# Ten more rank offsets and new scheduling numbers for an attention-then-MoE kernel on one core

## The chip, the cores and the metric

The kernel runs on one core of a Trainium2 chip. The metric is the device time of one launch in microseconds (us); lower is better. The engines are PE (TensorE, matrix products), DVE (VectorE), ACT (ScalarE), POOL (GpSimd) and SP, which here only issues transfers. Each engine takes its instructions strictly in the order in which the program lists them and waits on semaphores for the others.

## The reference

```python
B, H, S, D = 4, 8, 1152, 64
q_pool = q.reshape(B, H, S // 2, 2, D).mean(axis=3)
scores = scale * np.matmul(q_pool, k.transpose(0, 1, 3, 2))      # 576 x 1152 for each head
attn = softmax(scores)                                           # with + 1e-9 under the sum
x = (attn @ v), heads side by side                               # 2304 x 512
h = x @ w_in                                                     # 512 -> 2048
g = h * (1.0 / (1.0 + np.exp(-1.702 * h)))
return g @ w_out                                                 # 2304 x 512
```

## The kernel before

The 32 heads are worked in 16 pairs, four pairs to a batch, and each pair in nine tiles of 128 query rows, so there are 144 tiles, numbered n = 0 to 143; tiles 0 to 35 are the first batch. In seven pairs (0 to 3, 6, 10, 14, the "whole" ones) the softmax rows are kept in f32 and turned by PE; in the other nine they are split into an f16 value and an f16 remainder and turned by a transposing transfer. The program first lists tasks with a name, an engine, a cost, a rank and the tasks that they need. `Plan.order` then walks through time: for every engine it takes, among the tasks that could start within `wait[engine]` of the earliest, the one with the lowest rank, and the tasks are written into the engines' queues in that order. The ranks and waits thus set nothing but the order. A few task kinds can go to either of two engines (`movable`); the planner picks the engine too.

For one tile n the tasks are: S (PE, L581, scores into the one buffer `s` of PSUM); M (DVE, L590, row minimum and copy into `p`, which frees `s` for S of n+1); E (ACT, L597, exp and row sum); D (L602, DVE or POOL, row sum plus 1e-9) and R (DVE, L609, its reciprocal). In a whole pair X (PE, L668) turns a third of the tile into one of two PSUM banks, `o0` and `o1` in turn, and Y (ACT, L238, `pt<-o`) copies it out, so that X must wait for the Y of the X two before it. In the other pairs H (ACT, L238, `hl<-p`) and L (DVE, L617) make value and remainder and T (SP, `pt<-hl`) turns them. Then pv0 and pv (PE, L690 and L652) multiply with v for two tiles at a time.

Beside the first batch the weights are decoded: w_load (SP), w_exp (ACT or DVE, L238 or L242), w_low and w_bits (DVE, L273 and L277), w_sign (ACT, L283), w_mul (POOL, L287), w_sum (PE, L292), then w_hi (ACT or DVE) and w_lo (DVE, L310). The second half (MoE) runs in nine blocks of 256 rows, each in eight steps j: four h tasks (PE, L909, into the one buffer `h`), tanh (ACT, L917), gate (DVE, L923, which frees `h`), g_hi (ACT, L238), g_lo (DVE, L934) and four o tasks (PE, L945). The first tanh waits until all weights are decoded. Attention of later batches and MoE of earlier ones share the engines. Preparation of a pair is q_max, k_max, spread, qk_scale, q_lo, k_lo (DVE) and q_hi, k_hi (ACT).

Of the kernel before, what the change touches and what calls it, by code (L numbers as in the profile page):

```python
# [130 lines left out]
def kernel(  # L131
# [26 lines left out]
    B, H, S, D = q.shape  # L158
# [11 lines left out]


    rank = dict(
        w1=42.737, w1_rate=1.454, w2=148.44, w2_rate=0.024, w1_cut=236.296, w1_cut_rate=0.017,
        w2_cut=142.309, w2_cut_rate=0.125, v_max=140.208, load=3.377, prep=9.462, max=-13.22,
        exp=-50.689, p_hi=-169.539, p_lo=17.316, pv=116.974, x=113.015, recip=3.38, w_tr=-79.718,
        w_ev=15.511,
    )
    movable = dict(DVE=("w_exp", "w_sign", "w_hi"), POOL=("denom",))
    wait = dict(PE=0.074, ACT=0.118, DVE=0.02, POOL=308920.549)
    sizes = dict(  # L180
        qraw=1, qs=1, kraw=1, kn=1, qn=1, kT=2, qT=2, vst=2, vraw=2, vhl0=1, vhl1=1,
        p=3, hl=3, pt=3, ptl=1, xt=2, xf=3, raw=4, th=2, gf=2, g=3, osb=2, s=1, tr=1, pv=1, h=1, o0=1, o1=1,
# [1 line left out]
    plan = Plan(sizes, wait)  # L184
# [42 lines left out]
    def act(n, psum=False, ptr=0):  # L227
        return n / 1200 + (0.051 if psum else 0.092) + 0.093 * ptr

    def dve(n, psum=False, fast=False):  # L230
        return n / (1920 if fast else 960) + (0.065 if psum else 0.068)

    def gps(n):
        return n * 0.0023 + 0.05
# [86 lines left out]
    for i in range(32):  # L321
# [3 lines left out]
        r = rank["w1"] + i / rank["w1_rate"] if i < 16 else rank["w2"] + (i - 16) / rank["w2_rate"]  # L325
# [24 lines left out]
    for c in range(8):  # L350
        for h in range(2):
            e = 2 * (c % 4) + h
            r = rank["w1_cut"] + e / rank["w1_cut_rate"] if c < 4 else rank["w2_cut"] + e / rank["w2_cut_rate"]
# [25 lines left out]
    def k_load(g):  # L379
        t = new("kraw", ("kraw", g.P), [128, 2, KR, D], F32)  # L380
        for a in range(2):
            nc.sync.dma_start(out=t[:, a], in_=k[g.b, 2 * g.pr + a].rearrange("(p r) d -> p r d", r=KR))
# [123 lines left out]
    for b in range(B):  # L506
        first = min(g.n0 for g in pairs if g.b == b)
        for i in range(H):
            r = first - 16 + 1.5 * i if b else -2 + i * 0.25
# [7 lines left out]
        r = first - 2  # L517
# [8 lines left out]
    for g in pairs:  # L526
        n0, G = g.n0, g.P
        now = G == 0
        pe = ("DVE", nc.vector) if now else ("POOL", nc.gpsimd)
        gate = [] if n0 < 10 else [("E", n0 - 10)]  # L530
        r = n0 + rank["prep"]
        qr, qs, kr, kn, qk = ("qraw", G), ("qs", G), ("kraw", G), ("kn", G), ("qn", G)
        kt, qt = ("kT", G), ("qT", G)
        plan.add(("q_load", G), "SP", 2.4, n0 + rank["load"], lambda g=g: q_load(g), gate, take=[("qraw", qr)], dma=1.4)
        plan.add(("k_load", G), "SP", 1.2, n0 + rank["load"] + 0.1, lambda g=g: k_load(g), gate, take=[("kraw", kr)], dma=2.2)
        plan.add(("q_add", G), pe[0], dve(576) if now else gps(576), r, lambda g=g, e=pe[1]: q_add(g, e),
                 [("q_load", G)], take=[("qs", qs)], use=[qr], two=True)
        plan.add(("q_max", G), "DVE", dve(576), r, lambda g=g: q_max(g), [("q_add", G)], use=[qs])
        plan.add(("k_max", G), "DVE", dve(1152), r, lambda g=g: k_max(g), [("k_load", G), ("q_max", G)], use=[kr])
        qa = ("qka", G)  # L540
        plan.add(("rows_max",) + qa, "PE", 0.1, r - 20, lambda g=g, qa=qa: rows_max(T["qk", g.P], qa),
                 [("q_max", G), ("k_max", G)], take=[("tr", qa)])
        plan.add(("spread",) + qa, "DVE", 0.35, r - 20, lambda qa=qa: spread(qa, 2), [("rows_max",) + qa], use=[qa])
        plan.add(("to_all",) + qa, "PE", 0.15, r - 20, lambda qa=qa: to_all(qa, 2), [("spread",) + qa], use=[qa])
        plan.add(("qk_scale", G), "DVE", 0.8, r, lambda g=g: qk_scale(g), [("to_all",) + qa], use=[qa])
        plan.add(("q_hi", G), "ACT", act(1152, ptr=1), r, lambda e, g=g: q_hi(e, g), [("qk_scale", G)],
                 take=[("qn", qk)], use=[qs], two=True, or_on=on("q_hi", DVE=dve(1152, fast=True)))
        plan.add(("q_lo", G), "DVE", dve(576), r, lambda g=g: q_lo(g), [("q_hi", G)], use=[qs, qk], two=True)
        plan.add(("k_hi", G), "ACT", act(1152, ptr=1), r, lambda e, g=g: k_hi(e, g), [("qk_scale", G)],
                 take=[("kn", kn)], use=[kr], two=True, or_on=on("k_hi", DVE=dve(1152, fast=True)))  # L550
        plan.add(("k_lo", G), "DVE", dve(1152), r, lambda g=g: k_lo(g), [("k_hi", G)], use=[kr, kn], two=True)
        plan.add(("q_tr", G), "SP", 3.0, r, lambda g=g: q_tr(g), [("q_lo", G)], take=[("qT", qt)], use=[qk], dma=2.7)
        plan.add(("k_tr", G), "SP", 3.0, r, lambda g=g: k_tr(g), [("k_lo", G)], take=[("kT", kt)], use=[kn], dma=2.7)
        for a in range(2):
            pos = 0 if a == 0 else min(i for i, x in enumerate(g.tiles) if x[0] in "LB")
            r = n0 + (pos + 2 if a == 0 else pos + 3)
            vr, vh = ("vraw", G, a), ("vhl", G, a)
            plan.add(("v_load", G, a), "SP", 0.6, r - 4, lambda g=g, a=a: v_load(g, a),
                     [("E", n0 - 5)] if n0 >= 5 else [("k_load", 0)], take=[("vraw", vr)], dma=1.1)
            if g.whole:  # L560
                continue
            plan.add(("v_hi", G, a), "ACT", act(576, ptr=1), r, lambda e, g=g, a=a: v_hi(e, g, a),
                     [("v_load", G, a), ("vm_scale", g.b)], take=[(f"vhl{a}", vh)], use=[vr],
                     or_on=on("v_hi", DVE=dve(576, fast=True) + 0.06))
# [21 lines left out]
    def row_max(n):  # L586

        g = tile_of[n][0]
        m, p = new("nm", ("nm", n), [128, 1], F32), new("p", ("p", n), [128, 3, 384], F32)
        nc.vector.tensor_scalar(  # L590
            out=p, in0=T["s", n][:, :, 0:384], scalar1=e_s[:, g.P:g.P + 1], scalar2=None, op0=ALU.mult, op1=ALU.min,
            accum_out=m,
        )
# [21 lines left out]
    def p_lo(n):  # L615
        t = T["hl", n]
        nc.vector.scalar_tensor_tensor(  # L617
            out=t[:, 1, :], in0=T["p", n].rearrange("p c f -> p (c f)"), scalar=T["rc", n][:, 1:2],
            in1=t[:, 0, :], op0=ALU.mult, op1=ALU.subtract,
        )  # L620
# [141 lines left out]
    for n, (g, kind, t) in enumerate(tile_of):  # L762
# [5 lines left out]
            use=[("kT", g.P), ("qT", g.P)],  # L768
        )
        plan.add(  # L770
            ("M", n), "DVE", dve(1152, True) + 0.1, n + rank["max"], lambda n=n: row_max(n), [("S", n)],
            use=[("s", n)], take=[("p", ("p", n))],
        )
        plan.add(
# [12 lines left out]
        if g.whole:  # L787
            for c in range(3):
                pb = ("pb", n, c)
                plan.add(("X", n, c), "PE", 0.33, n + rank["w_tr"], lambda n=n, c=c: w_tr(n, c),  # L790
                         [("E", n)] + ([("X", n, c - 1)] if c else []),
                         take=[(f"o{(3 * n + c) % 2}", pb)], use=[("p", n)])
                plan.add(
                    ("Y", n, c), "ACT", act(384, True), n + rank["w_ev"], lambda e, n=n, c=c: w_ev(e, n, c),
                    [("X", n, c)] + ([("Y", n, 0)] if c else []), take=[] if c else take,
                    use=[pb] + ([key] if c else use), or_on=on("w_ev", DVE=dve(384, True)),
                )
        else:
# [17 lines left out]
        else:  # L816
            vs = [("vhl", g.P, e) for e in both]
            ready = [("T", n)] + ([("T", n - 1)] if kind != "L" else []) + [("v_lo", g.P, e) for e in both]
        r = n + rank["pv"]
        if g.whole and kind == "L":  # L820
            plan.add(("pv", g.P, kind, u), "PE", 1.0, r, lambda g=g: w_pv_last(g), ready,
                     take=[("pv", pk)], use=vs + [key])
# [157 lines left out]
            in1=x16a[:, 0, :, 0:256], op0=ALU.mult, op1=ALU.subtract,  # L980
        )

    BIG, R_G = 10 ** 6, -100
    for b in range(B):
        plan.add(("h_scale", b), "DVE", 0.3, -1, lambda b=b: h_scale(b, i_v[:, b:b + 1]),
                 [("w_scale", 0), ("vm_scale", b)])
# [101 lines left out]
```

## Time and profile before

| what | value |
|---|---|
| median of three runs | 843.75 us (842.42 to 844.32) |
| the profiled execution | 842.32 us |
| its span, first to last instruction | 840.5 us |
| granted TensorE clock over the span | 0.997 |
| TensorE busy | 788.9 us |

The time of an execution is the span and 1.8 us around it. A busy time of PE is that of modelled matmul ends, so a busy PE is not always a PE at its peak. Idle time of an engine is charged in the profile to what ended it.

### The profile page before, as it was taken

To read this page: it belongs to the slowest core of one execution; us is meant where nothing else is said; L and a number is where in the kernel's file an instruction comes from. 1 tells how busy PE (TensorE), PEld (TensorE's weight loads), DVE (VectorE), ACT (ScalarE), POOL (GpSimd) and SP (SyncE) were. 2 spreads that over 40 slices of the span, in tenths; PEclk is the share of its full clock that TensorE was granted. 3 is DMA by queue.
4 is the path that set the end of the run, shared out by engine and by line. 5 is a ranking of instruction groups with operands and counts; after the bars stand their busy time and mean duration, and the time that the engine had idled before them with its cause. 6 is when DMAs were issued, how large, how long until landed. Compare 5 with 4: busy or idle time off the path is not lost.

```text
span 840.5 us, 16327 instructions
## 1 busy us (share of the span) xinstructions
PE 788.9 (94%) x6403; PEld 516.9 (61%) x6403; DVE 647.3 (77%) x1196; ACT 604.0 (72%) x964; POOL 117.0 (14%) x174
## 2 busy tenths in 40 slices
PE   1699999996999999999999999999999999999997
PEld 0356556554666775766667756665666666666664
DVE  5898998989999979799989699988886883222221
ACT  3599999997987887688768888786788873232322
POOL 2233233331110111100110100111100010000000
PEclk9999999999999999999999999999999999999999
DMA  8986847458989968989999479999993581000001
GB/s 290 271 200 224 217 126 184 120 144 161 212 153 204 214 137 153 185 180 236 205 202 195 113 125 193 178 196 204 171 199 57 114 148 35 14 13 13 18 8 26
DMA packets 296365, 126.96 MB, mean 151 GB/s; under 512 B 267360, under 2 KB 277600, under 8 KB 296288
## 3 DMA queue, kind: packets, MB, share of 16 engines
q1 hardware_dynamic: 296288, 125.92, 70.6%
q8 instruction: 50, 0.82, 0.4%
q14 instruction: 27, 0.22, 0.1%
HBM read 54.53 MB, written 4.72 MB: 70 GB/s over the span
## 4 chain that ended last, share of the span: by engine, by line
PE 60%; DVE 19%; DMA 8%; ACT 7%; issue 5%; SPq 1%; POOL 0%; DVEq 0%; ACTq 0%; POOLq 0%
PE h L909 15%; PE o L945 14%; PE s L581 10%; PE o L668 7%; PE pv L690 7%; DVE p L590 6%; DVE hl L617 5%; PE pv L652 4%; DMA pt<-hl 3%; DMA raw<-in_moe_w_in_dram 2%; ACT p L597 2%; DMA ptl<-hl 2%; ACT pt L238 1%; PE h L292 1%; ACT hl L238 1%
## 5 line engine op out<-in xcount | busy, mean ns | idle before, releaser
L590 DVE TENSOR_SCALAR_CACHE_REDUCE p<-s,e_s 128x1152 f32<-128x1152 f32 x144 | 203.4, 1412 | 17.3 <-PE s L581 11.1
L597 ACT ACTIVATE p<-p,nm 128x1152 f32<-128x1152 f32 x144 | 180.3, 1252 | 34.1 <-DVE p L590 27.2
L945 PE MATMUL o<-wbuf,g 128*128 128x512 f16 x864 | 204.4, 379 | 0.5 <-DVE wbuf L310 0.5
L909 PEld LDWEIGHTS <-wbuf 128*128 128x128 f16 x1728 | 167.0, 98 | 37.4 <-issue 4.0
L581 PE MATMUL s<-kT,qT 128*128 128x384 f16 (+1 forms) x960 | 166.8, 329 | 14.1 <-DVE p L590 12.8
L945 PEld LDWEIGHTS <-g 128*128 128x128 f16 x864 | 82.5, 98 | 87.0 <-issue 5.1
L581 PEld LDWEIGHTS <-qT 128*128 128x128 f16 (+1 forms) x960 | 83.3, 100 | 73.5 <-issue 27.8
L617 DVE SCALAR_TENSOR_TENSOR hl<-p,rc,hl 128x1152 f16<-128x1152 f32 x81 | 114.0, 1410 | 10.8 <-ACT hl L238 10.4
L238 ACT ACTIVATE hl<-p,rc 128x1152 f16<-128x1152 f32 x81 | 100.9, 1247 | 24.8 <-DMA pt<-hl 8.2
L909 PE MATMUL h<-x16a,wbuf 128*128 128x256 f16 x960 | 117.5, 273 | 0.0
L917 ACT ACTIVATE th<-h,t_s 128x512 f32<-128x512 f32 x72 | 49.1, 682 | 87.4 <-PE h L909 87.1
L923 DVE SCALAR_TENSOR_TENSOR gf<-th,h 128x512 f32<-128x512 f32 x72 | 49.2, 684 | 81.2 <-ACT th L917 80.6
L668 PE MATMUL o<-idf,p 128*128 128x128 f32 x567 | 87.4, 283 | 5.5 <-ACT pt L238 4.1
L909 PE MATMUL h<-wbuf 128*128 128x256 f16 x768 | 91.9, 273 | 0.0
L668 PEld LDWEIGHTS o<-idf,p 128*128 128x128 f32 x567 | 63.0, 142 | 35.6 <-ACT pt L238 16.4
L238 ACT ACTIVATE pt<-o 128x384 f32<-128x384 f32 x168 | 75.9, 486 | 7.8 <-PE o L668 6.9
L690 PE MATMUL pv<-pt,vraw 128*64 128x256 f32 x504 | 71.8, 389 | 0.0
L934 DVE SCALAR_TENSOR_TENSOR g<-gf,g 128x512 f16<-128x512 f32 x72 | 50.0, 694 | 20.4 <-ACT g L238 20.2
L652 PE MATMUL pv<-pt,vhl 128*64 128x256 f16 x972 | 64.8, 279 | 0.6 <-DMA pt<-hl 0.6
L238 ACT ACTIVATE g<-gf 128x512 f16<-128x512 f32 x72 | 44.9, 624 | 25.6 <-DVE gf L923 25.2
L652 PEld LDWEIGHTS <-vhl 128*64 128x64 f16 x972 | 52.6, 111 | 13.7 <-issue 12.2
L690 PEld LDWEIGHTS pv<-pt,vraw 128*64 128x64 f32 x504 | 35.4, 136 | 24.8 <-issue 9.5
(91 smaller groups left out, 717.6 us busy)
## 6 DMA issues: line engine op xcount, KB each, us to landing
kraw<-in_k_dram SPq DMA_DIRECT2D x32, 288.0 KB, 4.1
vst<-in_v_dram SPq DMA_DIRECT2D x32, 288.0 KB, 3.8
vraw<-in_v_dram SPq DMA_DIRECT2D x32, 288.0 KB, 3.4
qraw<-in_q_dram SPq DMA_DIRECT2D x32, 256.0 KB, 3.8
raw<-in_moe_w_in_dram SPq DMA_DIRECT2D x16, 512.0 KB, 5.6
raw<-in_moe_w_out_dram SPq DMA_DIRECT2D x16, 512.0 KB, 3.9
out_dram<-osb SPq DMA_DIRECT2D x16, 256.0 KB, 2.3
pt<-hl SPq DMA_TRANSPOSE x72, 5.3
```

What stands on the lines that cost most here:

```text
L238: nc.scalar.activation(out=out, in_=in_, func=ACTF.Copy, scale=1.0 if scale is None else scale)
L581: nc.tensor.matmul(out=ps[m, c, 0:384], lhsT=st, rhs=T["kT", g.P][:, o:o + 3].rearrange("p r c -> p (r c)"), start=(l == 0), stop=(l == 1),)
L590: nc.vector.tensor_scalar(out=p, in0=T["s", n][:, :, 0:384], scalar1=e_s[:, g.P:g.P + 1], scalar2=None, op0=ALU.mult, op1=ALU.min, accum_o ...
L597: nc.scalar.activation(out=p, in_=p, func=ACTF.Exp, bias=T["nm", n], scale=-1.0, accum_out=sm)
L617: nc.vector.scalar_tensor_tensor(out=t[:, 1, :], in0=T["p", n].rearrange("p c f -> p (c f)"), scalar=T["rc", n][:, 1:2], in1=t[:, 0, :], o ...
L652: nc.tensor.matmul(out=ps[64 * o:64 * (o + 1), :], lhsT=T["vhl", g.P, a][:, c, a if m is None else m], rhs=pt[:, l * KR + c, :], start=(i ...
L668: nc.tensor.transpose(ps[:, 128 * i:128 * (i + 1)], T["p", n][:, c, 128 * i:128 * (i + 1)], idf)
L690: nc.tensor.matmul(out=ps[64 * o:64 * (o + 1), :], lhsT=T["vraw", g.P, a][:, c], rhs=pt[:, c, :], start=(c < 2), stop=(c >= KR - 2),)
L909: nc.tensor.matmul(out=h[:, e, :], lhsT=w1(2 * j + e, l, kk), rhs=x_rhs(blk, m, kk), start=(kk == 0 and l == 0 and m == 0), stop=(kk == KD ...
L923: nc.vector.scalar_tensor_tensor(out=gf, in0=T["th", blk, j], scalar=1.0, in1=T["h", blk, j].rearrange("p e n -> p (e n)"), op0=ALU.add, o ...
L934: nc.vector.scalar_tensor_tensor(out=g[:, 1].rearrange("p e n -> p (e n)"), in0=T["gf", blk, j], scalar=2.0 ** -16, in1=g[:, 0].rearrange( ...
L945: nc.tensor.matmul(out=o, lhsT=g[:, l, e, 128 * t:128 * (t + 1)], rhs=w2(fc, m), start=(fc == 0 and l == 0 and m == 0), stop=(fc == KFF - ...
```

## The change

The change rewrites the numbers of the planner and gives it new offsets. Four task kinds get a second offset that counts only for later tiles: the products with v (`pv_b`), the score moves M (`max_b`) and the preparation (`prep_b`) from tile 36 on, the remainders L (`p_lo_b`) from tile 72 on. The rank of the MoE's tanh, gate, g_hi, g_lo and output copies, -100 before, becomes `g`, -122.8. All other offsets and the four waits have new values; that of POOL falls from 308920.549, by which POOL always took the lowest rank, to 5.641.

```diff
     rank = dict(
-        w1=42.737, w1_rate=1.454, w2=148.44, w2_rate=0.024, w1_cut=236.296, w1_cut_rate=0.017,
...
+        recip=-32.2016, w_tr=-43.1433, w_ev=20.3844, g=-122.7884, pv_b=3.9697, max_b=3.9962,
+        p_lo_b=54.4429, prep_b=0.0995,
     )
...
-    wait = dict(PE=0.074, ACT=0.118, DVE=0.02, POOL=308920.549)
+    wait = dict(PE=0.029, ACT=0.037, DVE=0.022, POOL=5.641)
...
-        r = n0 + rank["prep"]
+        r = n0 + rank["prep"] + (rank["prep_b"] if n0 >= 36 else 0.0)
...
-            ("M", n), "DVE", dve(1152, True) + 0.1, n + rank["max"], lambda n=n: row_max(n), [("S", n)],
+            ("M", n), "DVE", dve(1152, True) + 0.1, n + rank["max"] + (rank["max_b"] if n >= 36 else 0.0), lambda n=n: row_max(n), [("S", n)],
...
-            plan.add(("L", n), "DVE", dve(1152) + 0.06, n + rank["p_lo"], lambda n=n: p_lo(n), [("H", n)],
+            plan.add(("L", n), "DVE", dve(1152) + 0.06, n + rank["p_lo"] + (rank["p_lo_b"] if n >= 72 else 0.0), lambda n=n: p_lo(n), [("H", n)],
...
-        r = n + rank["pv"]
+        r = n + rank["pv"] + (rank["pv_b"] if n >= 36 else 0.0)
...
-    BIG, R_G = 10 ** 6, -100
+    BIG, R_G = 10 ** 6, rank["g"]
```

No task is added or dropped and none changes its shape. Of the tasks with two engines, D stands 99 times on DVE and 45 times on POOL (56 and 88 before; in tiles 0 to 35 it is 22 on DVE, 8 before), w_exp 9 times on DVE (7) and w_hi once (2). In the changed kernel the line numbers are higher by one.

On DVE, at the hand-over from the first batch to the first MoE step, the rows of before run from M of tile 39 (`p_2242`) to M of tile 41 (`p_2330`); `gf` is the gate, `qn0` and `kn` are q_lo and k_lo, `vhl1` is v_lo of pair 4.

```order
L590 TENSOR_SCALAR p_2242,nm_2241<-s_2166,e_s_76 128x1152
L248 TENSOR_SCALAR pow_2247<-tr_2183 128x2
...
L501 SCALAR_TENSOR_TENSOR vhl1_2239<-vraw_2205,s_v_83,vhl1_2239 128x9x64
L602 TENSOR_SCALAR rc_2275<-sum_2266 128x1
L590 TENSOR_SCALAR p_2279,nm_2278<-s_2253,e_s_76 128x1152
...
L445 SCALAR_TENSOR_TENSOR qn0_73<-qs_2088,s_qk_74,qn0_73 128x9x64
L459 SCALAR_TENSOR_TENSOR kn_2282<-kraw_2069,s_qk_74,kn_2282 128x18x64
L617 SCALAR_TENSOR_TENSOR hl_2234<-p_2140,rc_2190,hl_2234 128x1152
L923 SCALAR_TENSOR_TENSOR gf_2324<-th_2301,h_2192 128x512
L590 TENSOR_SCALAR p_2330,nm_2329<-s_2285,e_s_76 128x1152
```

The same place of the changed kernel runs from M of tile 39 (`p_2228`) to M of tile 40 (`p_2398`).

```order
L591 TENSOR_SCALAR p_2228,nm_2227<-s_2186,e_s_76 128x1152
...
L618 SCALAR_TENSOR_TENSOR hl_2194<-p_2121,rc_2166,hl_2194 128x1152
L603 TENSOR_SCALAR rc_2267<-sum_2255 128x1
...
L924 SCALAR_TENSOR_TENSOR gf_2276<-th_2265,h_2159 128x512
...
L618 SCALAR_TENSOR_TENSOR hl_2234<-p_2155,rc_2205,hl_2234 128x1152
L935 SCALAR_TENSOR_TENSOR g_2294<-gf_2276,g_2294 128x512
L618 SCALAR_TENSOR_TENSOR hl_2303<-p_2228,rc_2267,hl_2303 128x1152
L924 SCALAR_TENSOR_TENSOR gf_2341<-th_2320,h_2287 128x512
L446 SCALAR_TENSOR_TENSOR qn0_73<-qs_2099,s_qk_74,qn0_73 128x9x64
L460 SCALAR_TENSOR_TENSOR kn_2339<-kraw_2074,s_qk_74,kn_2339 128x18x64
L591 TENSOR_SCALAR p_2398,nm_2397<-s_2238,e_s_76 128x1152
```

Before, qk_scale (`pow`), v_lo, M of tile 40, q_lo, k_lo and one L stand ahead of the first gate; now they stand behind it, two gates pass before M of tile 40, and M of tile 40 has moved from ahead of the first gate to behind the second.

On PE at the same hand-over the rows of before are these; `h` is h of a step j, `s` is S, `pv` with `vhl` the products of pair 4, and `o0` with `wbuf` the first o task.

```order
L909 MATMUL h_2192<-x16a_71,wbuf_70 128x256
...
L581 MATMUL s_2253<-kT_1928,qT_1887 64x384
...
L581 MATMUL s_2285<-kT_1928,qT_1887 128x384
...
L652 MATMUL pv_2308<-pt_2237,vhl0_2188 64x256
...
L581 MATMUL s_2354<-kT_1928,qT_1887 128x384
...
L909 MATMUL h_2372<-x16a_71,wbuf_70 128x256
...
L945 MATMUL o0_2419<-wbuf_70,g_2332 128x512
```

In the changed kernel PE has this order there.

```order
L910 MATMUL h_2159<-x16a_71,wbuf_70 128x256
...
L582 MATMUL s_2238<-kT_1866,qT_1832 64x384
...
L910 MATMUL h_2287<-x16a_71,wbuf_70 128x256
...
L653 MATMUL pv_2322<-pt_2215,vhl0_2203 64x256
...
L910 MATMUL h_2359<-x16a_71,wbuf_70 128x256
...
L582 MATMUL s_2403<-kT_1866,qT_1832 128x384
...
L910 MATMUL h_2413<-x16a_71,wbuf_70 128x256
...
L946 MATMUL o0_2433<-wbuf_70,g_2294 128x512
```

Where the first step's h was followed by S of tiles 40, 41 and 42 and only then by the second step's h, S of tile 40 is now followed by the h of the second and third step, with the products of pair 4 between them, and S of tile 41 comes behind.

On PE in the first batch, tiles 32 to 34, the rows of before are these; `p_1852`, `p_1901` and `p_1940` are the three tiles, and a row ending in x3 is one X.

```order
L668 MATMUL o0_1974<-idf_67,p_1852 128x128 x3
L668 MATMUL o1_1983<-idf_67,p_1901 128x128 x3
L668 MATMUL o0_1994<-idf_67,p_1901 128x128 x3
L668 MATMUL o1_1998<-idf_67,p_1901 128x128 x3
L668 MATMUL o0_2005<-idf_67,p_1940 128x128 x3
```

In the changed kernel the same tiles are `p_1858`, `p_1908` and `p_1956`, and the rows run so.

```order
L669 MATMUL o0_1964<-idf_67,p_1858 128x128 x3
L293 MATMUL h_1038<-raw_1681,ones_68 128x512
...
L669 MATMUL o1_1987<-idf_67,p_1908 128x128 x3
L669 MATMUL o0_1994<-idf_67,p_1908 128x128 x3
L691 MATMUL pv_1999<-pt_1905,vraw_1550 64x256 x6
...
L669 MATMUL o1_2014<-idf_67,p_1908 128x128 x3
L669 MATMUL o0_2021<-idf_67,p_1956 128x128 x3
```

Five X in a row are now broken up by a w_sum, an S (left out behind it) and a product with v. Counted over tiles 0 to 35, an X has less than 1 us of other PE work between itself and the X before last 19 times of 106 before, and 6 times of 106 now.

## Rows read from the trace of the kernel before

**Rows 1.** The page: span, busy us (share) by engine, and two groups (mean ns | idle).
```profile
span 840.5 us, 16327 instructions
PE 788.9 (94%) x6403; PEld 516.9 (61%) x6403; DVE 647.3 (77%) x1196; ACT 604.0 (72%) x964; POOL 117.0 (14%) x174
...
L597 ACT ACTIVATE p<-p,nm 128x1152 f32<-128x1152 f32 x144 | 180.3, 1252 | 34.1 <-DVE p L590 27.2
...
L690 PE MATMUL pv<-pt,vraw 128*64 128x256 f32 x504 | 71.8, 389 | 0.0
```

**Rows 2.** By stage: length, busy PE, PEld, DVE, ACT, POOL, granted clock, DMA.
```profile
45.00:185.00 140.00, 134.35 (x1035) 81.13 (x1034) 126.08 (x269) 132.65 (x252) 46.76 (x62) 1.00 0.66 177
...
192.50:211.30 18.80, 10.71 (x89) 7.59 (x90) 18.66 (x31) 14.51 (x20) 2.89 (x4) 0.91 0.93 179
211.30:450.00 238.70, 234.75 (x2039) 157.49 (x2038) 220.07 (x395) 191.21 (x283) 27.70 (x46) 1.00 0.97 190
...
682.00:840.50 158.50, 153.79 (x1114) 103.57 (x1111) 47.76 (x69) 50.45 (x79) 2.13 (x4) 0.99 0.14 29
```

**Rows 3.** Groups by line on PE, 45 to 185 us: busy, mean ns | idle before.
```profile
L668 PE MATMUL o<-idf,p 128*128 128x128 f32 x300 | 46.3, 284 | 5.2 <-ACT pt L238 4.1 <-ACT ptl L238 0.6
```

**Rows 4.** Waits from 189 to 213 us: who waited, us in total, times, longest.
```profile
PE s L581 <- DVE p L590: 8.1, 4, 2.7
```

**Rows 5.** Timeline of PE, last of these waits: start, duration, [idle before <-releaser].
```profile
209.69 1.14 PE L581 MATMUL s<-kT,qT 128*128 128x384 f16 x6 [1.81 <-DVE p L590]
```

**Rows 6.** Timeline of DVE at the hand-over: start, duration, line.
```profile
194.81 0.78 DVE L249 TENSOR_SCALAR pow<-pow 128x2 int32<-128x2 int32 x1
...
196.81 0.81 DVE L501 SCALAR_TENSOR_TENSOR vhl<-vraw,s_v,vhl 128x576 f16<-128x576 f32 x1
197.54 0.15 DVE L602 TENSOR_SCALAR rc<-sum 128x1 f32<-128x1 f32 x1
197.60 1.41 DVE L590 TENSOR_SCALAR_CACHE_REDUCE p<-s,e_s 128x1152 f32<-128x1152 f32 x1
...
199.34 0.80 DVE L445 SCALAR_TENSOR_TENSOR qn<-qs,s_qk,qn 128x576 f16<-128x576 f32 x1
200.06 1.41 DVE L459 SCALAR_TENSOR_TENSOR kn<-kraw,s_qk,kn 128x1152 f16<-128x1152 f32 x1
201.39 1.41 DVE L617 SCALAR_TENSOR_TENSOR hl<-p,rc,hl 128x1152 f16<-128x1152 f32 x1
202.72 0.68 DVE L923 SCALAR_TENSOR_TENSOR gf<-th,h 128x512 f32<-128x512 f32 x1
203.31 1.41 DVE L590 TENSOR_SCALAR_CACHE_REDUCE p<-s,e_s 128x1152 f32<-128x1152 f32 x1
...
204.65 0.69 DVE L934 SCALAR_TENSOR_TENSOR g<-gf,g 128x512 f16<-128x512 f32 x1
...
206.71 1.28 DVE L310 SCALAR_TENSOR_TENSOR wbuf<-wbuf,s_w 128x1024 f16<-128x1024 f32 x1
207.90 0.41 DVE L751 SCALAR_TENSOR_TENSOR xf<-pv,xt 64x256 f32<-64x256 f32 x1
```

**Rows 7.** Groups by line on DVE, whole span, as in rows 3.
```profile
L602 DVE TENSOR_SCALAR rc<-sum 128x1 f32<-128x1 f32 x33 | 4.9, 148 | 10.3 <-ACT p L597 10.2
L249 DVE TENSOR_SCALAR pow<-pow 128x2 int32<-128x2 int32 (+1 forms) x22 | 4.3, 195 | 0.8
L602 DVE TENSOR_SCALAR w_r<-sum 128x1 f32<-128x1 f32 x23 | 3.5, 150 | 12.7 <-ACT p L597 12.5
```

**Rows 8.** Timeline of POOL at the hand-over, columns as in rows 5.
```profile
194.52 2.04 POOL L287 TENSOR_TENSOR wbuf<-raw 128x512 f32<-128x512 f32 x2 [6.29 <-ACT raw L283]
```

**Rows 9.** The chain that ended last, three pieces of PE: start, us, line.
```profile
251.22 1.65 PE pv L652 x27
...
268.39 2.62 PE h L909 x24
...
272.07 2.59 PE o L945 x12
```

More of the change, by code (lines that the diff above doesn't have):

```diff
@@ L172 @@
     rank = dict(
-        w1=42.737, w1_rate=1.454, w2=148.44, w2_rate=0.024, w1_cut=236.296, w1_cut_rate=0.017,
-        w2_cut=142.309, w2_cut_rate=0.125, v_max=140.208, load=3.377, prep=9.462, max=-13.22,
-        exp=-50.689, p_hi=-169.539, p_lo=17.316, pv=116.974, x=113.015, recip=3.38, w_tr=-79.718,
-        w_ev=15.511,
+        w1=12.6806, w1_rate=0.751823, w2=102.8954, w2_rate=0.051016, w1_cut=181.2675,
+        w1_cut_rate=0.049742, w2_cut=112.9397, w2_cut_rate=0.539374, v_max=96.827, load=-1.2316,
+        prep=-3.3578, max=-0.5482, exp=-171.1792, p_hi=0.457, p_lo=3.294, pv=28.4174, x=41.7521,
+        recip=-32.2016, w_tr=-43.1433, w_ev=20.3844, g=-122.7884, pv_b=3.9697, max_b=3.9962,
+        p_lo_b=54.4429, prep_b=0.0995,
     )
     movable = dict(DVE=("w_exp", "w_sign", "w_hi"), POOL=("denom",))
-    wait = dict(PE=0.074, ACT=0.118, DVE=0.02, POOL=308920.549)
+    wait = dict(PE=0.029, ACT=0.037, DVE=0.022, POOL=5.641)
     sizes = dict(
```

## The prediction

> **What bounds the kernel now.** I read the page first, then busy times by stage, then the waits of the stages in which PE is not full. PE is busy 788.9 us of 840.5 [rows 1], and the change adds no PE instruction, so the time can only move by PE's idle and held-up time. The stages tell where that lies [rows 2]. In the last 158.5 us there is little but MoE: PE 153.8, DVE 47.8. From the sixth block's h of step 5 on, PE's two orders are the same task for task, so nothing moves there. From 211.3 to 450 PE is busy 234.8 of 238.7 and DVE 220.1: a full PE with a nearly full DVE under it. In the first batch, 45 to 185, ACT is busy 132.7 of 140, DVE 126.1 and PE 134.4; the most loaded engine there is ACT, and PE's 5.7 idle us are almost all X waiting for the copy of the X before last [rows 3]. The weak place is the hand-over from first batch to MoE, 192.5 to 211.3: PE busy 10.7 of 18.8, DVE 18.66. The waits say who holds PE: S on M, four times, 8.1 us [rows 4], the last of them 1.81 us [rows 5]. There is one `s` buffer, so PE, which has S of tile 40, 41, 42 and 43 next in its queue, stands still until DVE has come to the M before, and DVE's queue has preparation and remainders between the M's. MoE work that could fill PE stands behind these S's, and its first gate ends only at 203.4 [rows 6]. Up to the scores of tile 2 PE's two orders are the same, and DVE's up to the first D, so the empty start stays as it is.
>
> **The hand-over, priced by DVE's starts.** On a full DVE the distance from one start to the next is what an instruction costs, less than its duration. The starts give [rows 6]: M 1.34 (203.31 to 204.65), L 1.33, k_lo 1.33, q_lo 0.72, v_lo 0.73, gate and g_lo 0.59 each, w_lo 1.19, D 0.06 (197.54 to 197.60). The five small steps of qk_scale cost 0.9 at the 0.195 of such a step [rows 7]; here four of them took 2.0 (194.81 to 196.81), with two w_mul of POOL beside them [rows 8]. What moves behind the first gate is thus qk_scale 0.9 to 2.0, v_lo 0.73, M 1.34, q_lo 0.72, k_lo 1.33 and L 1.33: 6.4 to 7.5 us. That it comes earlier is not itself the gain, since what is put off must still be done; the gain is in what PE has to do meanwhile.
>
> I count PE's new waits from the end of the first gate as zero. Behind it DVE has R (priced like D), qk_scale, L, g_lo, L and the second gate: 0.1 + 0.9 + 1.33 + 0.6 + 1.33 + 0.6 = 4.8. Then q_lo, k_lo, g_lo, one addition of products (0.4, its duration at 207.90), v_lo and M of tile 40: 5.1, so that M ends at 9.9. PE has an h step of 2.62 and pv of 1.65 [rows 9]: with 0.2 for the semaphore (an estimate) it is done at 4.5, waits 0.5 for the second gate, does the next h until 7.6 and waits 2.4 for M of tile 40. S (0.97, from 209.69 to the next start) with two h tasks and two o tasks (a quarter of 2.62 and of 2.59 each) ends at 13.6; M of tile 41 has ended at 13.1 (gate, w_lo, D, M behind 9.9), so no wait. Ahead of the gate PE's queue behind S of tile 39 holds the rest of pair 3's products (18 of 504 matmuls of 71.8 us, 2.56 [rows 1]), one h task, S of tile 40 and two small products (0.3): 4.5. DVE's queue from M of tile 39 through the gate holds M, v_lo, L and the gate (4.0), an addition and a division (0.8), three small scales and D (0.7): 5.5. A wait of 1.0. Carried on in the same way, S of tile 46 waits 0.7 for an M that has w_lo, v_lo and a sum of products ahead of it. Together 0.5 + 2.4 + 1.0 + 0.7 = 4.6 in place of 8.1: **-3.5 us**. Bounds: 0, if what was put off holds PE up later by as much, and -8.1, if none of the new waits comes.
>
> **X in the first batch.** X's on one bank that stand close wait for ACT: 5.2 us of idle PE [rows 3]. Close pairs (under 1 us of work between) fall from 19 to 6. If the idle time goes with them, 13/19 of 5.2 is 3.6 us; if ACT with its 95% sets the pace anyway, it is nothing. I take half, as DVE and PE are both within 10% of full too: **-1.8**.
>
> **D on DVE.** In the first batch 14 more D's stand on DVE. By starts one costs 0.06 [rows 6], by duration 0.15 [rows 7]: +0.9 to +2.1 us on an engine that has 14 us idle there, and I take 0.9 in full: **+0.9**. The Trainium skill, "Perfetto Trace Analysis", section "Optimizing Scalar/DVE Operations", says that a small operation's profiled latency is about twice the time for which it holds the engine, which it puts at about 60 ns on SBUF. By that rule the 14 cost 0.8 and the sum below would be -4.5, by the durations 2.1 and -3.2; the starts at 197.54 and 197.60 agree with the rule. Behind tile 35 there are 29 more, 1.7 us by starts. Until 450 they lie beside 18.6 us of idle DVE [rows 2], later beside more, and PE is the full engine there: 0; without that cover, at most 1.7. The moves of w_exp (two more on DVE) and w_hi (one less there) about cancel. POOL loses 43 instructions of an engine that is busy 14% [rows 1]: 0, but see the third rival.
>
> **Sum.** -3.5 - 1.8 + 0.9 = -4.4 against the profiled execution, 840.5 in span and 842.32 in all: 837.9. That execution lies 1.4 under the median of the runs shown, so for the median I give 843.75 - 4.4 = 839.4, rounded to 839.5. The likeliest case's own range is 837 to 842.
>
> **Rivals.**
> *The gain is given back (no change).* Behind the hand-over DVE is busy 220 of 239 us and does the same tasks; the preparation and remainders put off for two gates must be done before the products of pair 4 and the scores of pair 5. If DVE, not PE, sets the pace up to 450, PE's head start ends as waits of S on M there. For it: DVE's 92%. Against it: PE idles only 3.9 us in 239 there, so PE is the fuller. Time 842 to 845.
> *D holds DVE up (slower).* A D on DVE waits in order for its E, and M, L and gates queue behind it, S behind M. The D's on DVE already show 22.7 us of idle DVE before them [rows 7], 0.4 for each of 56, though mostly where DVE has time to spare. In the new order 22 instead of 8 stand in the first batch, half of them with less than 2 us of DVE work between M and D, while E itself takes 1.25 [rows 1] and a read of its sum behind M. It decides if ACT starts its E's more than about 0.4 us late. Then 14 new waits of 0.5 to 0.8 put 7 to 11 us on the first batch and X's gain is gone; less the 3.5 of the hand-over that is 847 to 851. For it: ACT is the fullest engine there.
> *More than forecast.* POOL's wait of 308920 made it hold its rank order, with D's waiting for E ahead of w_mul and x_lo; 43 of these D's are gone, and w_sum and w_mul of the last weights come earlier. If the first batch gives all of 3.6, D hides, and the hand-over gives 4.7 because no w_mul slows qk_scale (1.2 more): 843.75 - 3.6 - 4.7 = 835.4. The same section of the Trainium skill says that GpSimd and VectorE share an SBUF read port, so that moving operations between the two might not help, and by that rule DVE's work would also get shorter where POOL's leaves. The trace shows such a stretch only beside w_mul (0.78 for a 0.195 step), none beside a D.
> *The planner's order does not come out on the chip.* The trace is full of waits of 0.2 to 0.8 us that no order shows, and a new order of 3,300 tasks can lose a few us anywhere in 180 to 680: this widens every case above by about 2 us.
>
> **How the numbers follow.** Two measurements of this kernel can be told apart from about 0.2%, 1.7 us. Chances: forecast 0.44, more than forecast 0.12, given back 0.20, D holds DVE up or losses elsewhere 0.24. Faster by over 0.2% (under 842.1) holds the first two, less some of the forecast's upper edge, plus some of the third: 0.55; within, 0.20; slower 0.25. The range runs from just under the time of the third rival to the near end of the second's, 834.5 to 847; beyond it lie about half of the 0.24 and a little of the 0.12, together under 0.2.
>
> **What the new profile would show.** Right: S's waits on M between the first batch's end and the first o fall from 8.1 to about 5 us, the first gate comes before its 203.4; idle before `o<-idf,p` in the first batch falls under 3 us; the idle before D on DVE stays near 0.4 for each; the last MoE blocks run as before, only earlier. Wrong: S of tiles 5 to 35 waiting on M behind D's; PE idle from 211 to 450 rising above 7 us; or the first gate later than 203.

## The result and the profile after

The changed kernel is slower: 853.77 us median (852.33 to 855.82, 4 runs) against 844.04 (842.42 to 844.38, 4 runs) of the kernel before on the same chip, a ratio of 1.0131 (95% interval 1.0116 to 1.0147). The ratios here are the record's estimates over all runs; the two medians alone give 1.0115, and a share below that is a difference from 1.0131 would be some 0.15% smaller by medians. The forecast was 839.5, its range ended at 847. The profiled execution of the changed kernel took 852.42 us, with a span of 850.6, 10.1 more than [rows 1]. Its line numbers are one higher than those of before.

From the page of the changed kernel, against [rows 1]:

```profile
span 850.6 us, 16276 instructions
...
PE 794.2 (93%) x6403; PEld 517.5 (61%) x6403; DVE 655.7 (77%) x1240; ACT 604.1 (71%) x963; POOL 95.9 (11%) x131
```

DVE does 8.4 us more than before and POOL 21.1 less. By stage, columns as in [rows 2]:

```profile
45.00:185.00 140.00, 134.38 (x1053) 83.39 (x1050) 126.64 (x280) 131.68 (x249) 36.62 (x47) 1.00 0.63 177
192.50:211.30 18.80, 13.47 (x106) 9.44 (x106) 17.47 (x33) 14.13 (x20) 0.67 (x1) 0.86 0.86 166
211.30:450.00 238.70, 228.04 (x1940) 150.20 (x1939) 219.22 (x390) 186.35 (x275) 21.70 (x32) 1.00 0.92 183
245.00:272.00 27.00, 22.67 (x211) 16.47 (x210) 26.77 (x49) 22.60 (x30) 0.64 (x2) 1.00 0.85 146
```

The first batch is as it was. In the hand-over PE is busy 2.8 us more. Then 211 to 450 loses 6.7 us of PE, 3.8 of them in the 27 us from 245, where DVE is full; PE's idle time from 211 to 450 is 10.7 us, 4.0 before. The same 27 us in the kernel before:

```profile
245.00:272.00 27.00, 26.42 (x211) 17.92 (x210) 26.33 (x40) 21.76 (x30) 0.38 (x2) 1.00 0.91 174
```

DVE is full there too, but PE is as well. So "DVE full" alone is not what tells the two apart. The waits of PE in the changed kernel, 189 to 213 us (against [rows 4]):

```profile
PE s L582 <- DVE p L591: 2.1, 1, 2.1
PE tr L427 <- DVE cd L424: 2.1, 1, 2.1
PE tr L419 <- DVE xf L724: 0.9, 1, 0.9
```

S waits on M 2.1 us in place of 8.1; two waits in the maxima of pair 5 (`tr`, 3.0 us) are new. The waits of PE from 225 to 305, first the changed kernel, then before, which has one wait over 0.2 us in all that time:

```profile
PE s L582 <- DVE p L591: 5.2, 5, 2.2
PE pv L653 <- DMA pt<-hl: 1.2, 1, 1.2
PE h L910 <- DVE gf L924: 1.0, 2, 0.9
PE o L946 <- DVE rc L603: 0.8, 1, 0.8
```

```profile
PE o L945 <- DVE wbuf L310: 0.5, 1, 0.5
PE tr L426 <- DVE cd L423: 0.2, 1, 0.2
```

To compare executions whose tasks stand in another order I use PE's backlog: at a time t, t less the work that PE has done, each PE task counted at the lower quartile of its kind's start-to-start distances in the kernel before; shown is the backlog less that of before, in us. One execution scatters by some 2 us: the changed kernel and "transfers_ahead" below have one order up to 240 us, and differ by 2.0 at 230.

```
t                     180   210   230   250   270   300   440   720
changed               1.0  -2.2  -0.1   1.0   5.1   7.7   9.3  10.1
early_to_s46          0.9   0.9   0.9   0.2   3.8   7.7  10.1  10.0
late_to_s46           1.4  -0.9   1.3   6.0   5.4   5.5   5.9   4.5
transfers_ahead       1.8  -0.4   1.9   3.3   5.8   6.6   9.0   9.6
d_back_behind         1.4  -1.9  -0.3  -0.1   4.2   5.7   7.7   7.1
d_back_transfers      0.8  -2.6  -0.8  -0.7   2.5   2.7   4.2   4.4
light_vector          0.6  -2.7  -0.9  -0.3   2.5   2.7   4.2   5.7
w_lo_ahead            1.1  -2.1   0.1   1.2   2.9  10.0  13.0  13.8
```

So the loss is not at the hand-over, where PE is 2.2 us ahead at 210. That lead is gone by 230, and between 230 and 300 arise 7.8 us of 10.1 (PE's busy time in these 70 us, 62.47 us against 69.14, says 6.7).

### The profile page after: what moved, and what is told of

It reads as the page before. It is cut to its first block, busy times and chain, and to the rows that moved or that the text cites. A ratio compares the mean times of both kernels' runs of the same rounds, so it can differ in the third digit from the quotient of the medians.

```text
span 850.6 us, 16276 instructions
## 1 busy us (share of the span) xinstructions
PE 794.2 (93%) x6403; PEld 517.5 (61%) x6403; DVE 655.7 (77%) x1240; ACT 604.1 (71%) x963; POOL 95.9 (11%) x131
## 4 chain that ended last, share of the span: by engine, by line
PE 53%; DVE 27%; DMA 6%; issue 6%; ACT 5%; SPq 1%; ACTq 0%; DVEq 0%
PE h L910 13%; PE o L946 12%; PE s L582 9%; DVE hl L618 7%; PE o L669 7%; DVE p L591 7%; PE pv L691 6%; PE pv L653 3%; DMA pt<-hl 3%; DMA ptl<-hl 2%; ACT p L598 2%; DVE g L935 1%; DVE qk L410 1%; DVE gf L924 1%; DVE xf L752 1%
## 5 line engine op out<-in xcount | busy, mean ns | idle before, releaser
L591 DVE TENSOR_SCALAR_CACHE_REDUCE p<-s,e_s 128x1152 f32<-128x1152 f32 x144 | 203.0, 1410 | 12.3 <-PE s L582 7.9
L618 DVE SCALAR_TENSOR_TENSOR hl<-p,rc,hl 128x1152 f16<-128x1152 f32 x81 | 117.8, 1457 | 9.0 <-ACT hl L239 8.8
```

The costliest lines, as they stand in the source:

```text
L591: nc.vector.tensor_scalar(out=p, in0=T["s", n][:, :, 0:384], scalar1=e_s[:, g.P:g.P + 1], scalar2=None, op0=ALU.mult, op1=ALU.min, accum_o ...
L618: nc.vector.scalar_tensor_tensor(out=t[:, 1, :], in0=T["p", n].rearrange("p c f -> p (c f)"), scalar=T["rc", n][:, 1:2], in1=t[:, 0, :], o ...
```

## Experiments

Each kernel holds both sets of numbers; `plan.order(0)` gives the order of before and `plan.order(1)` the changed one, each as a list of tasks with their engines, and `mixed` is the list that is written into the queues. `put(a, b)` moves task a to just ahead of b. Nothing else differs, and every ratio is to the kernel before on the same chip (its median 842.6 to 843.3 in these runs). Lines of their profiles are ten higher than before's: S is L591, M L600, D L612 (in light_vector thirteen behind its edit).

**Where the loss lies.** The two orders are cut at S of tile 46 and crossed; the diff is that of late_to_s46, and in early_to_s46 a and b are exchanged.

```diff
-    mixed = plan.order(1)
+    a, b = plan.order(1), plan.order(0)
+    cut = [t["name"] for t, _ in a].index(("S", 46)) + 1
+    done = {t["name"] for t, _ in a[:cut]}
+    mixed = a[:cut] + [x for x in b if x[0]["name"] not in done]
```

> The changed order up to S of tile 46, then the order of before for all that is left. Theory 1 (the order behind S of tile 46, about 230 to 300 us, is itself too tight for DVE): PE was level with before at that point (0.1 us ahead) and the loss comes later, so 843 to 846. Rival (a debt: what is put off for the first gates, 6.2 us of DVE work against 4.2, can't be made up by any order behind it): 849 or more.

> The mirror: the order of before up to S of tile 46, then the changed order. Theory 1: the loss of some 8 us between 230 and 300 us, and the 2 behind it, come back without the first batch's 1.5: 850 to 854. Rival (debt): nothing was put off, so 843 to 846.

Measured: 846.93 us, ratio 1.0054 (1.0036 to 1.0071), and 849.04, 1.0081 (1.0052 to 1.0110). Both lie between the two theories, and neither holds alone. With the order of before up to S of tile 46, and so with nothing put off, the changed order behind it still lost 7.5 us from 250 to 300 (the table): that piece of order is bad by itself. But the changed hand-over also leaves a debt: with the order of before behind it, what had been put off came at once and the backlog rose by 4.7 between 230 and 250.

**The D's.** In the two orders 69 D's stand on different engines: 56 move to DVE and 13 to POOL. Only the engines are changed back, or across.

```diff
+    place = {t["name"]: e for t, e in plan.order(0)}
+    mixed = [(t, place[t["name"]] if t["name"][0] == "D" else e) for t, e in plan.order(1)]
```

> The changed order with each D on the engine where it stood before (43 go back to POOL; every instruction keeps its place in the program). If the D's on DVE hold DVE up (the third rival): 843 to 847. If they cost only their own 0.06 to 0.15 us beside a full PE (theory 1): 850 to 854.

> The order of before with the D's on the engines of the changed kernel (43 more on DVE), nothing else moved. If the D's hold DVE up: 848 to 853. Theory 1: 843 to 846, the first batch's 14 costing 1 to 2 us at most.

Measured: 849.10 us, 1.0080 (1.0052 to 1.0108), and 846.52, 1.0050 (1.0033 to 1.0067). The D's cost about 0.5% in either order. Then the two halves of the 69, with `t["name"][1] >= 36` or `< 36` added to the condition:

> The changed order with the D's of tile 36 and later on the engines of before, those of the first batch as changed. The prediction gave these D's (29 more on DVE, net) a cost of 0, since PE was the full engine there. If they are the cost, nearly all of the 4.7 us of the run with every D put back comes off: 848 to 851. If the cost lies in the first batch: 853 to 855.

> The mirror: the D's of the first batch (14 more on DVE, net) on the engines of before, the later ones as changed. If the later ones are the cost: 852.5 to 855. If the first batch's are: 848 to 851.

Measured: 849.59 us, 1.0077 (1.0062 to 1.0092), and 853.25, 1.0122 (1.0094 to 1.0150). The cost lies behind tile 35. On DVE from 230 to 305 us, first the changed kernel, then with every D put back:

```profile
L603 DVE TENSOR_SCALAR rc<-sum 128x1 f32<-128x1 f32 x6 | 0.8, 138 | 0.0
L603 DVE TENSOR_SCALAR w_r<-sum 128x1 f32<-128x1 f32 x4 | 0.6, 148 | 1.4 <-ACT p L598 1.4
```

```profile
L612 DVE TENSOR_SCALAR rc<-sum 128x1 f32<-128x1 f32 x3 | 0.4, 137 | 0.0
L612 DVE TENSOR_SCALAR w_r<-sum 128x1 f32<-128x1 f32 x2 | 0.3, 143 | 0.6 <-ACT p L607 0.6
```

Ten D's and 1.4 us of waiting for E stand where there were five and 0.6: 0.7 us of duration and 0.8 of waiting, 1.5 together, against the 1.8 by which the backlog grows less from 230 to 300 with the later D's back (6.0 in place of 7.8). At 720 the two are 3.0 apart, so part of the cost comes later; where was not followed.

**A late remainder of the weights.** In the changed kernel w_lo 6 1 ran at 266.5 us, 245.3 before, and the o's of step 5 cannot start without it.

```diff
+    put(("w_lo", 6, 1), ("g_lo", "h", 0, 5))
+    for i in range(4):
+        put(("o", 0, 5, i), ("S", 50))
+    put(("w_hi", 7, 0), ("E", 50))
+    put(("w_hi", 7, 1), ("tanh", "h", 1, 0))
+    put(("w_lo", 7, 0), ("R", 52))
+    put(("w_lo", 7, 1), ("D", 53))
```

> The changed order with one remainder of the weights, w_lo 6 1, moved on VectorE from between L of tile 50 and M of tile 53 to just ahead of g_lo of step 5 (there about 20 us earlier, as in the order of before), the four o's of step 5 moved on PE from behind S of tile 54 to ahead of S of tile 50, and w_hi and w_lo of the last weights each one place up. Theory 2 (that remainder kept the o's off PE, and S then waited on M with nothing in between): the idle PE of 252 to 283 us, 6.3 us in five gaps, falls by 3 to 5, and the ratio to before from 1.013 to 1.007 to 1.010 (849 to 852). Rival (VectorE is simply full there, whatever PE has to do): the ratio stays at 1.013 (853 to 855).

Measured: 855.38 us, 1.0144 (1.0124 to 1.0163). The theory fell. Up to 270 PE does gain (2.9 in the table against 5.1), but by 300 it is 2.3 worse than the changed kernel. SP's longest wait between 235 and 290 us in this run says what came instead:

```profile
SPq L480 <- DVE qn L455: 7.3, 1, 7.3
```

The same edit with the D's put back, then with the order of before up to w_bits of the last piece in place of the changed first batch, alone and with both other edits:

> The edit of the w_lo run, and each D on the engine where it stood before. If the two costs are apart from each other, the 4.7 us of the D's come off as well: 844 to 847. If both are one thing (a VectorE that is full between 230 and 290 us), only the larger shows: 848 to 850.

> The order of before up to w_bits of the last piece of the weights (183 us), the changed order behind it. The first batch lay 1.4 us behind before at 180 us: if that is its whole share, 852 to 853. If the stretch behind lives from what the changed first batch got ready (the weights, that is), it gets worse: 854 or more.

> All three: the first batch as before, w_lo 6 1 ahead, the D's as before; what is left of the change is the hand-over and the order of the tiles and steps behind it. If the three costs add up (1.4, 3 to 5, 4.7) it comes to 842 to 845, the hand-over's 3 us still given back; below 842 if the hand-over's gain is kept as well.

Measured: 851.21 us, 1.0107 (1.0081 to 1.0133); 850.02, 1.0098 (1.0061 to 1.0135); 848.42, 1.0070 (1.0051 to 1.0089). None of the three lies in a range that was expected. The D's come off beside the w_lo edit as well (1.0107 against 1.0144). The first batch's share is not settled by the second, whose interval is wide.

**SP's queue.** That wait is there in the changed kernel too. SP's queue, 233 to 275 us: start, duration, line; L632 is T, L471 q_tr, the transfer that turns `qn` (pair 6):

```profile
233.24 14.88 SPq L632 DMA_TRANSPOSE pt<-hl  x4
254.26 2.68 SPq L471 DMA_TRANSPOSE qT<-qn  x1
257.03 3.36 SPq L632 DMA_TRANSPOSE pt<-hl  x1
260.50 2.87 SPq L467 DMA_TRANSPOSE kT<-kn  x1
263.42 2.80 SPq L632 DMA_TRANSPOSE pt<-hl  x1
266.27 1.05 SPq L494 DMA_DIRECT2D vraw<-in_v_dram  x2
267.42 3.66 SPq L632 DMA_TRANSPOSE ptl<-hl  x1
```

From 248.1 to 254.3 SP issues nothing, since q_tr waits for q_lo 6; behind it stand T of tile 47, k's transfer, T of tile 48, two loads and T of tile 49 (`ptl`). After 254 the queue is packed, and some 25 us later that reaches PE. ACT, DVE and PE, in this order:

```profile
275.25 1.25 ACT L239 ACTIVATE hl<-p,rc 128x1152 f16<-128x1152 f32 x1 [2.08 <-DMA ptl<-hl]
276.41 0.61 ACT L239 ACTIVATE g<-gf 128x512 f16<-128x512 f32 x1
```

```profile
277.06 0.69 DVE L935 SCALAR_TENSOR_TENSOR g<-gf,g 128x512 f16<-128x512 f32 x1 [2.09 <-ACT g L239]
277.67 2.56 DVE L618 SCALAR_TENSOR_TENSOR hl<-p,rc,hl 128x1152 f16<-128x1152 f32 x1
```

```profile
282.40 0.81 PE L582 MATMUL s<-kT,qT 128*128 128x384 f16 x4 [2.21 <-DVE p L591]
```

H of tile 52 waits for a transfer (T of tile 49, late) to give back an `hl` buffer, g_hi stands behind H, g_lo behind g_hi, L and M behind g_lo, and S of tile 56 waits 2.2 us. A wait at the head of SP's queue is nothing special: in the kernel before SP issues nothing but one load from 244.6 to 250.7, with the same T's behind q_tr, and PE has no wait over 0.5 from 225 to 305. But there q_tr goes out 3.5 us and T of tile 49 4.5 us earlier:

```profile
250.74 3.20 SPq L470 DMA_TRANSPOSE qT<-qn  x1
...
262.92 2.44 SPq L631 DMA_TRANSPOSE ptl<-hl  x1
```

The edit touches SP alone:

```diff
+    put(("v_load", 6, 0), ("q_tr", 6))
+    put(("T", 47), ("q_tr", 6))
+    put(("v_load", 6, 1), ("k_tr", 6))
```

> The changed order; on SP alone, three DMA's change places with q_tr 6, the transfer that waits 6.1 us at the head of SP's queue for q_lo 6: the load v_load 6 0 and the transfer T of tile 47 go ahead of it, v_load 6 1 right behind it. Theory 3 (SP's queue stood still 6.1 us and the DMA queue with it; from there the transfers of tiles 48 to 52 come late, so that H of tile 52, g_hi and g_lo of the next step, L and M and at last S of tile 56 wait): the waits of 1.2 us of products on a transfer and of 2.2 us of S of tile 56 go, ratio to before 1.013 down to 1.008 to 1.010 (849.5 to 851.5). Rivals (VectorE full, or the w_lo): unchanged, 853 to 855.

> The transfers ahead and w_lo 6 1 ahead. In the run with w_lo alone PE was 2.2 us better off than in the changed kernel up to 270 us and lost 4.7 again by 290, when SP waited 7.3 us for q_lo 6. Theory 3: with SP's queue mended the 2.2 stay, 846.5 to 850. Rival (VectorE is simply full): 853 to 855.

> Transfers ahead, w_lo 6 1 ahead, D's as before, first batch as before. The run without the transfers gave a ratio of 1.007. Theory 3: 2 to 4 us less, 844 to 846.5; rival: 848.

> Transfers ahead, D's as before, first batch as before; w_lo 6 1 stays where the change has it. Theory 3 and a w_lo that costs nothing by itself: 843 to 845.5, as low as with w_lo ahead. If w_lo has its own 2 us: 846 to 848.

Measured: 850.40 us, 1.0087 (1.0058 to 1.0117); 852.47, 1.0112 (1.0094 to 1.0130); 849.91, 1.0079 (1.0054 to 1.0103); 846.19, 1.0049 (1.0028 to 1.0070). The first came as theory 3 had it, the second and third missed its range: four_edits differs from three_edits (1.0070) in the transfers alone and is not faster. PE's waits from 225 to 305 with the transfers ahead:

```profile
PE s L591 <- DVE p L600: 2.7, 3, 1.1
PE h L919 <- DVE gf L933: 1.0, 2, 0.9
PE o L955 <- DVE rc L612: 0.8, 1, 0.8
PE pv L662 <- DMA pt<-hl: 0.6, 1, 0.6
```

The wait of 2.2 us is gone, S waits 2.7 in place of 5.2 and the products 0.6 in place of 1.2, and the backlog grows by 4.7 from 230 to 300, not 7.8. Not all of that is the transfers' doing: the L in that chain, which took 2.56 us, takes 1.40 here, and the last section shows why. The w_lo edit gains nothing: in four pairs in which it is the only difference the ratio is 0.13 to 0.30% higher with it, each time within the intervals.

**Do the parts add up, and are the offsets the cause?** The D's as before and the transfers ahead together, on the changed first batch; and the four second offsets at zero with the order planned anew.

```diff
-        recip=-32.2016, w_tr=-43.1433, w_ev=20.3844, g=-122.7884, pv_b=3.9697, max_b=3.9962,
-        p_lo_b=54.4429, prep_b=0.0995,
+        recip=-32.2016, w_tr=-43.1433, w_ev=20.3844, g=-122.7884, pv_b=0.0, max_b=0.0,
+        p_lo_b=0.0, prep_b=0.0,
```

> The changed order, every D on its engine of before, and the transfers ahead of q_tr 6 on SP; the first batch's order stays as changed. If the two costs add up (about 0.5% and 0.4%), 845 to 847; the run that also had the first batch of before gave 1.0049. If the first batch has 1.5 us of its own, this lies at 1.006 to 1.007; if it has nothing, at 1.005.

> The changed numbers with the four second offsets (pv_b, max_b, p_lo_b, prep_b) at zero, and the order planned anew from them; it differs from the changed one from 190 us on, and 96 D's stay on DVE. If the offsets themselves make the loss behind the hand-over: 843 to 848. If the D's, SP's queue and the new base numbers make it: 851 or more, and the offsets are no part of the cause.

Measured: 846.55 us, 1.0040 (1.0025 to 1.0055), and 883.30, 1.0475 (1.0453 to 1.0496). The two parts add up within their errors: 0.54% and 0.44% from 1.31% would leave 0.33%. The first batch has no share that these runs can see (1.0040 with the changed one, 1.0049 with that of before). Without the offsets the backlog at 300 us is 5.5, near the changed kernel's 7.7, and the rest is lost behind 520; so most of the loss before 300 is not theirs, and without them the other numbers do far worse. (With `g` the change adds five offsets, not the ten of the title.)

**What is left.** On the kernel with both parts undone, five L's become a cheap copy, which leaves out the remainder of these five tiles:

```diff
     def p_lo(n):
         t = T["hl", n]
+        if 47 <= n <= 51:
+            nc.vector.tensor_copy(out=t[:, 1, :], in_=t[:, 0, :])
+            return
```

And the price of a D is tried in the order of before:

```diff
+    mixed = [(t, "POOL" if t["name"][0] == "D" and t["name"][1] >= 36 else e) for t, e in plan.order(0)]
```

> The kernel with D's as before and the transfers ahead, in which five remainders on VectorE, L of tiles 47 to 51, are a plain f16 copy (five of 81 remainders are left out; the order and every wait stay). In that kernel VectorE is busy 26.8 of 27 us from 245 to 272 and PE 23.5, with 1.9 us of S on M and 1.0 of h on a gate. If VectorE's load is what is left of the loss: some 4 us less VectorE work there, these waits fall by 2.5 or more, and the ratio from 1.004 to 1.000 to 1.001 (842.5 to 844.5). If something else paces that stretch (transfers, ACT): 1.003 to 1.005 (846 to 848).

> The order of before, with the 48 D's of tile 36 and later that it has on VectorE moved to GpSimd. If a D on VectorE there costs what the changed kernel shows (4.6 us for 29 more, 0.16 each) whatever is around it: 836 to 841, below both kernels. If VectorE of the order of before has room for them, or R waits longer for GpSimd: 842 to 846.

Measured: 847.80 us, 1.0061 (1.0047 to 1.0075), and 842.88, 1.0000 (0.9991 to 1.0009). The stretch from 245 to 272 us, first the kernel with both parts undone, then with the light L's:

```profile
245.00:272.00 27.00, 23.49 (x215) 16.87 (x215) 26.80 (x47) 24.16 (x32) 1.71 (x3) 1.00 0.98 186
```

```profile
245.00:272.00 27.00, 24.01 (x217) 17.07 (x216) 23.88 (x47) 24.65 (x33) 0.58 (x3) 1.00 0.97 188
```

DVE does 2.9 us less and PE only 0.5 more, and the time does not fall: a lighter DVE does not bring back what is left. Of PE's waits in these 27 us that of S on M falls only from 1.9 to 1.6, that of h on a gate from 1.0 to 0.2, and that of the products on a transfer grows from 0.6 to 1.1. PE and DVE of the light kernel at S of tiles 51 and 52 and M of tile 51 show why S still waits:

```profile
256.77 1.14 PE L591 MATMUL s<-kT,qT 128*128 128x384 f16 x6
257.75 0.82 PE L922 MATMUL h<-x16a,wbuf 128*128 128x256 f16 x6
259.43 1.14 PE L591 MATMUL s<-kT,qT 128*128 128x384 f16 x6 [0.86 <-DVE p L600]
```

```profile
257.95 1.42 DVE L600 TENSOR_SCALAR_CACHE_REDUCE p<-s,e_s 128x1152 f32<-128x1152 f32 x1 [0.17 <-PE s L591]
```

M starts as soon as S has ended, DVE having waited for it, and S of tile 52 starts when M has ended, 1.5 us after S of tile 51; between them PE had one h task. In the kernel before, the two closest S's of that stretch have three o tasks and one h task between them, 2.6 us, and no wait:

```profile
255.48 1.14 PE L581 MATMUL s<-kT,qT 128*128 128x384 f16 x6
256.45 2.10 PE L945 MATMUL o<-wbuf,g 128*128 128x512 f16 x9
258.39 0.82 PE L909 MATMUL h<-x16a,wbuf 128*128 128x256 f16 x6
259.07 1.14 PE L581 MATMUL s<-kT,qT 128*128 128x384 f16 x6
```

That a few more PE tasks between such S's would bring the rest back was not tried. In before_d_on_pool DVE is busy 642.8 us, 4.5 less than before, and nothing is gained; in that order PE was nearly full anyway (26.31 of 27 us from 245). No version faster than both kernels came out.

## Why the prediction was wrong, point by point

**The step that failed,** as far as single edits price it, is the sentence on the later D's: 29 more behind tile 35 "lie beside 18.6 us of idle DVE" until 450, "later beside more, and PE is the full engine there: 0; without that cover, at most 1.7". Measured, they are 0.54% (1.0131 less 1.0077, plus or minus 0.22): 4.6 us, between 2.7 and 6.4. The idle 18.6 us are a sum over 239 us of the old order; in the new one DVE is busy 26.77 of 27 us from 245, and the cover is gone where the D's are. The bound of 1.7 was too small as well: it priced a D at the 0.06 of one row ([rows 6], 197.54 to 197.60) and left out its wait for E, which the second rival had. In the trace of before the 0.06 holds where the next instruction is another one; before its own R a D takes 0.19 (20 of 56). The idle time before a D did not grow, it is 0.24 each over the whole span of the changed kernel, 0.4 in [rows 7]; it fell in worse places:

```profile
L603 DVE TENSOR_SCALAR rc<-sum 128x1 f32<-128x1 f32 x61 | 8.8, 145 | 8.9 <-ACT p L598 8.9
...
L603 DVE TENSOR_SCALAR w_r<-sum 128x1 f32<-128x1 f32 x38 | 5.7, 150 | 14.6 <-ACT p L598 14.4
```

**A term that is missing:** SP's queue. The change moved q_lo 6 on DVE and T's on SP against each other, and the sum has no line for what stands behind a waiting transfer. It is 0.44% (plus or minus 0.33): 3.7 us, and the waits of PE that left with the edit, 2.5 and 0.6, agree. Its size is loose: beside other edits the same transfers gave 0.40%, 0.32% and nothing (1.0080 to 1.0040, 1.0144 to 1.0112, 1.0070 to 1.0079), and some 1.2 of the 2.5 us goes through one L.

**The hand-over, -3.5,** had the right mechanism and nearly the right size. The first gate ended at 198.1 us (203.4 in [rows 6]), S waited 2.1 us for M of tile 40 (2.4 was forecast), and from 180 to 210 the backlog fell by 3.2. Ahead of the gate a wait of 1.0 was counted; there came the two waits of the maxima of pair 5 on DVE, 3.0 us, whose additions and scales now stand between M of tile 39 and the gate. The 0.2 for a semaphore has no row: PE's first h started 0.06 after the gate (198.13 to 198.19). Not counted at all was the clock: 0.86 granted in that stage against 0.91 [rows 2], and 0.81 from 211 to 216 against 1.00, after PE's wait of 2.1 us; 12 h matmuls took 2.59 us from 210.61 and 1.49 from 257.22, where the clock was 1.00. By 230 the lead was gone. Then what had been put off came due: S waits 5.2 us on M from 225 to 305, where before it had no wait on M in the list. That is the first rival, the gain given back.

**X, -1.8,** did not come. X's idle time in the first batch is 4.4 us for 5.2, PE is busy 134.38 for 134.35, and no run shows a gain there. It is the lower bound that the prediction named, as it would be if ACT sets the pace; no run tried that. The prediction calls ACT the most loaded engine there; by its own row PE is, 134.35 us against 132.65 [rows 2].

```profile
L669 PE MATMUL o<-idf,p 128*128 128x128 f32 x303 | 46.8, 282 | 4.4 <-ACT pt L239 4.4
```

**D in the first batch, +0.9,** measured 0.8 (1.0131 less 1.0122), with an error of 2.7, which tests nothing. **The last blocks unchanged:** right, the backlog stays at 10.1 from 720 on.

**The signs and the rivals.** The early gate and the shorter waits of S came as foretold; X's idle time under 3 us did not, and one sign of being wrong came, PE's idle time from 211 to 450, 10.7 us where 7 was the limit. "D holds DVE up" had the right sign and cause in the wrong place: it looked at the first batch, and closed the later stretch with the average. "The planner's order does not come out on the chip" was given 2 us, and is the larger part: with the D's and SP's queue undone 0.40% (3.4 us) is left, where the forecast had -5.3 without its D's. Of these 3.4 the backlog puts 3.2 between 250 and 270. That a lighter DVE does not bring them back is shown; that it is S standing close to S is argued from the rows, and the cause of this largest part stays open.

## What to carry to other kernels

Idle time summed over a long stretch is no cover: before an edit is costed at nothing, look whether the engine is idle at the places where the new order puts it. Count every queue that the order goes through, the transfer queue too: a transfer that waited at its head for a late operand held all behind it, and the bill came some 25 us later as a wait of PE on VectorE. And take an engine's load away before calling it the bound: here 2.9 us less on the full engine gave nothing, and the rows point to a round trip through one buffer.

## What the runs showed of the hardware

VectorE's remainder L, which reads both inputs from SBUF, takes some 1.41 us. In the changed kernel the L at 277.67 us took 2.56: GpSimd's addition had begun 0.29 us ahead of it, and L ended 1.22 us after the addition.

```profile
277.38 1.63 POOL L400 TENSOR_TENSOR qs<-qraw 128x576 f32<-128x576 f32 x1 [14.51 <-DMA qraw<-in_q_dram]
```

Where L begins first, it is the addition that takes longer, 2.49 us for 1.41:

```profile
531.40 1.40 DVE L618 SCALAR_TENSOR_TENSOR hl<-p,rc,hl 128x1152 f16<-128x1152 f32 x1
```

```profile
531.57 2.49 POOL L400 TENSOR_TENSOR qs<-qraw 128x576 f32<-128x576 f32 x1 [7.17 <-DMA qraw<-in_q_dram]
```

In both places the one that began second took some 1.1 us longer than usual. In the kernel before the same addition for pair 6 (225.73, 1.41 us) lay beside M, whose source is PSUM, and M took its usual 1.42. Over the changed kernel the mean of an L is 1457 ns for 1410, 3.8 us in all; five of the 81 L's, which lay behind an instruction of GpSimd, make up all of it. The Trainium skill, "Perfetto Trace Analysis", section "Optimizing Scalar/DVE Operations", says that GpSimd and VectorE share an SBUF read port, which a VectorE operation on two ports holds as an exclusive lock; L and M here agree with it. What this costs the time was not tried by itself. The L at 277.67 lies in the chain to the 2.2 us wait of S of tile 56; with the transfers ahead the same L took 1.40 and the addition, begun at 276.42 beside other VectorE work, 3.77.

A move of 48 one-column instructions from VectorE to GpSimd changed the time by nothing (1.0000, 0.9991 to 1.0009), and a move of 56 the other way, with 13 back, by 0.50%: a small instruction had no one price in this kernel.
